# Earlier requests for the first unit's keys and queries, later copies of the first seeds, and a fourth tile for seeds

## The chip, the cores and the metric

The kernel runs on one core of a Trainium2 chip, as one program. The metric is the device time of one execution in microseconds (us). The core has five engines that run side by side: TensorE (PE in the profile; its weight loads are the row PEld), VectorE (DVE), ScalarE (ACT), GpSimd (POOL) and SyncE (SP). In this kernel SP does nothing but ask for DMA transfers, and all of them go through its one queue.

## The reference, cut to what matters

Two independent halves are computed and put side by side. Both have a sequence length of 2048 and a width of 448.

```python
# half A: a state space convolution
P = exp((A * dt)[:, :, None] * pos)           # 448 channels x 256 states x 2048 positions
K = 2 * einsum("dn,dnl->dl", C, P).real       # one filter per channel
y = irfft(rfft(u) * rfft(K))[:2048] + u * D_skip
# half B: attention with 16 heads of 28
q, k, v = split(x @ wqkv)
o = softmax(q @ k.T * 28**-0.5) @ v
out_b = o @ wo
```

## The kernel before, in words

The program has two stages. The first one, the projection stage (the program's loop `for t in range(n_stage)`, line 530), makes two things side by side:

- The products x @ wqkv, in 48 jobs: four chunks of 512 rows, and in each chunk the keys and queries of four groups of four heads and four pieces of v. A job (`qk_proj`, line 448) has 12 matmuls. Its result is split into a high and a low part, tile `hl` (two buffers), by one ACT and one DVE instruction, and stored in HBM (`k<-hl`, `q<-hl` in the profile). The split and the store of a job are written into the program after the matmuls of the job behind it. In the last chunk the keys and queries of group 0 come as jobs 40 and 41, of group 1 as 42 and 43, of group 2 as 44 and 45, of group 3 as 46 and 47.
- The seeds of the filters, from `seeds(o)` for o = 0 to 7 (line 313): few powers of the exponentials, for 7 blocks of 8 channels each. The first half of a set is built in a tile `se`, which is one of three buffers that carry the name `qhat`; POOL clears a part of it with a memset (`places`, line 359) and fills it, and `put_e` stores it (`sd<-qhat`). `put_g` stores the other half (`sd<-sg`).

The loop runs over steps t = 0 to 40. Step t takes the projection jobs that are due (all are done by t = 36), the pieces of the seeds of that step, and the requests in `ahead[t]`. Those requests are for the first attention unit (group 0, first 512 queries): its key differences `kdif` (`load_kd`, 16 transfers of 64 KB), its queries `qhat` (`load_q(0)`, four of 256 KB) and its keys `khat` (`load_k(0, j)`, one head j at a time, four of 256 KB for each). The buffer of the keys of group 0 holds the projection weights until then: the keys of head j lie where the weights of group j were.

After the loop come the maxima of unit 0: for each of 16 pieces of 128 queries, four matmuls (`max_mm`, line 173). The first is reduced by a Relu on ACT (tile `rl`), the second together with that tile by a DVE instruction, the third and fourth by one DVE reduction each. `max_join`, `max_end` and `max_put` write the result into the queries (`qhat<-mh`).

The second stage is the attention loop over 256 steps of 128 keys. In each step four score matmuls (`pss`) go to four exponentials on ACT (`p`) and four product matmuls (`po`). Woven into it are the maxima of the next unit, which run three pieces (LEAD) ahead, and half A: 56 blocks of filters. For a block b the seeds are loaded (`load_sd`, tile `sdb`), copied by ACT into tiles `e` and `g` (`k_seeds`, two calls), multiplied up to all powers by nine POOL instructions for `e` and nine steps on DVE for `g`, and joined by matmuls (`pm<-e,g`). `k_next` asks for the seeds of a later block once the powers of a block are done.

The order of instructions on an engine is set in two ways. In the projection stage and the maxima of unit 0 nothing is pinned (`KEPT["p"]` is empty): the framework's planner orders each engine's instructions by their place in the program and by when it reckons them ready. From line 861 on all five engines keep the order of the program. Tiles of one name share its buffers, and a new tile waits until the last use of the tile before it in that buffer is over.

Of the kernel before, what the change touches and what calls it, by code (L numbers as in the profile page):

```python
# [8 lines left out]
F32 = mybir.dt.float32  # L9
F32R = mybir.dt.float32r  # L10
I32 = mybir.dt.int32
AF = mybir.ActivationFunctionType
# [28 lines left out]
PS = 1  # L41
SGB, XB, XL = 2, 5, 4
K0, KP, KD, UP = 0, 3.5, 4, 3
A0, A1, KW = 26, 34, (33, 35, 36)

N1 = 32
N2 = 64
# [3 lines left out]
NB = D // 8  # L51
# [7 lines left out]
SDF = F_Z + 18 * 16  # L59
# [31 lines left out]
def body(ctx, tc, a, out):  # L91
    nc = Engines(tc)
# [4 lines left out]
    def pool(stack, name, bufs=1, space=None, side=None):  # L97
        kw = {} if space is None else {"space": space}
        if side:
            kw["side"] = side  # L100
        return stack.enter_context(tc.tile_pool(name=name, bufs=bufs, reuse_waits="tile", **kw))
# [31 lines left out]
    k0_p = pool(k0_st, "k0_p", side="right")  # L133
# [11 lines left out]
    def load_k(g, j, p):  # L145
        if j == 0:
            t = k0_t if g == 0 else p.tile([128, HG, L], F32R, name="khat")
            kt_g[g] = [t[:, i] for i in range(HG)]
        for r in range(4):
            nc.sync.dma_start(kt_g[g][j][32 * r:32 * r + 32, :].bitcast(F32), k_d[g][r % 2, 32 * j:32 * j + 32, :])  # L150
# [3 lines left out]
    def load_v(g, c):  # L154
        v_g[g, c] = t = v_p.tile([128, NK // NQ, HG, 32], F32, name="v", bufs=5)
        nc.sync.dma_start(t.rearrange("p t h e -> p t (h e)"), v_d[c][:, g])
# [8 lines left out]
    def load_q(u, rows=range(4)):  # L165
        g, c = divmod(u, NQ)
        if 0 in rows:
            q_u[u] = q_p.tile([128, HG, CQ], F32R, name="qhat", bufs=3)
        t = q_u[u]
        for r in rows:  # L170
            nc.sync.dma_start(t[32 * r:32 * r + 32].bitcast(F32), q_d[g][c][r // 2].rearrange("(j p) q -> p j q", j=HG))

    def max_mm(u, i, kc, ps=w_tile):

        if i == 0 and kc == 0:
            m_u[u] = q_p.tile([128, HG, 4, 3], F32, name="mx", bufs=2)
        j, t = divmod(i, 4)
        pm = ps()
        q, kt = q_u[u][:, j, t * 128:(t + 1) * 128], kt_g[u // NQ][j]
        mx = m_u[u][:, j, t, max(kc - 1, 0):max(kc - 1, 0) + 1]  # L180
        if kc == 0:
            nc.tensor.matmul(pm, q, kd_g[u // NQ, j], start=True, stop=True)
            rl_u[u, i] = kd_p.tile([128, CQ], F32, name="rl", bufs=2)
            nc.scalar.activation(rl_u[u, i], pm, AF.Relu)
        elif kc == 1:
            kb = kt.rearrange("p (c s n) -> p c s n", c=NQ, s=2)[:, :2, 1, :]
            nc.tensor.matmul(pm.rearrange("p (c n) -> p c n", c=2), q, kb, start=True, stop=True)
            rl = rl_u.pop((u, i))
            nc.vector.tensor_tensor_reduce(rl, pm, rl, 1.0, -3.0e38, ALU.add, ALU.max, mx)
        else:  # L190
            nc.tensor.matmul(pm, q, kt[:, kc * CQ:(kc + 1) * CQ], start=True, stop=True)
            nc.vector.tensor_reduce(mx, pm, axis=AX.X, op=ALU.max)

    def max_join(u):
        m_u[u, 1] = q_p.tile([128, HG * 4], F32, name="m1", bufs=2)
        nc.vector.tensor_reduce(m_u[u, 1], m_u[u].rearrange("p a b c -> p (a b) c"), axis=AX.X, op=ALU.max)

    def max_end(u, ps):
        nc.tensor.transpose(ps[:16, :128], m_u[u, 1], ident)
        mh = q_p.tile([16, 2, 128], F32R, name="mh")  # L200
        nc.vector.tensor_scalar(mh[:, 0, :], ps[:16, :128], -1.0, None, op0=ALU.mult)
        nc.vector.scalar_tensor_tensor(mh[:, 1, :], ps[:16, :128], -1.0, mh[:, 0, :].bitcast(F32),
                                       op0=ALU.mult, op1=ALU.subtract)
        mh_u[u] = mh
# [7 lines left out]
    with ExitStack() as st:  # L212
# [47 lines left out]
        t = a["A_log_dt"]  # L260
# [6 lines left out]
        half_pi = s_p.tile([128, 1], F32, name="half_pi")  # L267
# [245 lines left out]
        ahead = collections.defaultdict(list)  # L513
# [2 lines left out]
        for i in range(2):  # L516
            ahead[A1 + i].append(lambda i=i: load_q(0, range(2 * i, 2 * i + 2)))

        for j, t in enumerate(KW):
            ahead[t].append(lambda j=j: load_k(0, j, k0_p))  # L520

        def project():

            e = work.pop(0)() if work else None
            while pend:
                pend.pop(0)()
            if e:
                pend.append(e)

        for t in range(n_stage):  # L530
            while work and n_work - len(work) < n_work * (t + 1) / PW:
                project()
            for f in slots[t] + ahead.get(t, []):
                f()
            if t + 1 == PW:
                project()
                wst.close()
                load_k(0, HG - 1, k0_p)
                load_q(1)
                for c in range(NQ):  # L540
                    load_v(0, c)
        xst.close()
        more = [lambda: ps_t.tile([128, CQ], F32, name="pt")] * 2 + [w_tile] * 3
        for i in range(16):
            for kc in range(4):
                max_mm(0, i, kc, more[(4 * i + kc) % 5])
        max_join(0)
        max_end(0, ps_t.tile([128, CQ], F32, name="pt"))
        max_put(0)
# [6 lines left out]
    g_p = pool(g_st, "g_p")  # L556
# [56 lines left out]
    sds, egs = {}, {}  # L613

    def load_sd(b):
        sds[b] = g_p.tile([128, SDF], F32, name="sdb", bufs=3)
        nc.sync.dma_start(sds[b], sd_d[b // BO][b % BO])

    def k_seeds(b):

        if b not in es:
            es[b] = e = g_p.tile([128, 2, 16, N2], F32, name="e", bufs=2)
            nc.scalar.activation(e[:, :, :, :8], sds[b][:, :F_G].rearrange("p (c h e) -> p c h e", c=2, e=8), AF.Copy)
        else:
            g = g_p.tile([128, 2, 16, N1], F32, name="g", bufs=2)
            nc.scalar.activation(g[:, :, :, :4], sds[b][:, F_G:F_Z].rearrange("p (c h e) -> p c h e", c=2, e=4), AF.Copy)
            egs[b] = es.pop(b), g
# [231 lines left out]
        return spectrum(f, i, p, uh_p, ps, b0) if kind == "s" else finish(f, i, p, ps, b1)  # L859

    nc.kept = KEPT["a"]
    load_sd(0)
    load_sd(1)
    k_seeds(0)
    k_seeds(0)
    for i in range(LEAD):
        for kc in range(4):
            max_mm(1, i, kc)

    urgent, back = collections.deque(), collections.deque()  # L870
    powers = {"g": collections.deque(), "e": collections.deque()}
# [113 lines left out]
    last = [None]  # L985

    def k_next():

        if last[0] is not None and not powers["e"] and not powers["g"]:
            if last[0] + 2 < NB:  # L990
                load_sd(last[0] + 2)
            last[0] = None

    def vec():
# [4 lines left out]
    for s in range(NS):  # L999
# [26 lines left out]
        for op in ORDER:  # L1026
            if op[0] == "s":
                ps.append(s_mm(u, kt, int(op[1])))
            elif op[0] == "f":
                slot(s)  # L1030
            elif op[0] == "v":
                vec()
            elif op == "k":
                k_next()
                k_begin(s)
                k_seed(s)
                for _ in range(3):
                    if powers["e"]:
                        powers["e"].popleft()()
            elif op == "pv":  # L1040
                if prev:
                    pv_step(*prev)
                    if prev[1] == NK - 1:
                        fin(prev[0], s)
            elif sm < NS:
                max_mm(sm // NK, sm % NK, int(op[1]))
        for _ in range(FX if late[0] else 0):
            slot(s)
        if sm < NS and sm % NK == NK - 1:
# [3 lines left out]
            max_join(sm // NK)  # L1053
            soon_slot(UG[0], end)
        k_next()
        prev = (u, kt, ps)
    pv_step(*prev)
# [65 lines left out]
```

## Time and profile before

| | us |
|---|---|
| median of three runs | 1332.18 |
| lowest and highest | 1330.11 and 1336.95 |
| the profiled execution | 1331.76 |
| its span, first to last instruction | 1329.9 |

The span lies 1.9 us below the profiled execution's own time. All instructions are recorded on one line of the code (L75, a helper), so they are told apart by their tiles: `hl<-pm` is what writes tile `hl` from tile `pm`. In the timelines a row has the start and the length in us, the engine, the operation, the tile that is written and those that are read, the shapes and a count; in brackets stands the idle time of that engine before it, and what ended it. SPq is SP asking for a transfer, not the transfer itself.

### The profile page before, as it was taken

The numbers are of one execution on the slowest core, as the hardware profiler recorded it, in microseconds if no ns is written. First come the engines' busy times: TensorE is split into PE (matmuls) and PEld (weight loads), VectorE is DVE, ScalarE is ACT, GpSimd is POOL, SyncE is SP. The second block draws the span as 40 slices with busy tenths as digits, with TensorE's granted clock in tenths as the row PEclk, the third lists the DMA queues.
The fourth block names the chain that finished last, engine by engine and source line by source line (L and its number), as shares of the span: only waits on it lengthen the run. The fifth ranks groups of instructions, "written<-read, shape, count | busy, mean of one in ns | idle before, by whom it ended". The sixth has DMA issues, their size and how long they took to land.

```text
span 1329.9 us, 33195 instructions
## 1 busy us (share of the span) xinstructions
PE 1235.2 (93%) x12625; PEld 705.0 (53%) x12625; DVE 990.1 (74%) x2138; ACT 953.2 (72%) x2067; POOL 838.4 (63%) x704
## 2 busy tenths in 40 slices
PE   6878885699999999999999999999999999898997
PEld 5656763355555555555555555555555545444433
DVE  5897786787777887787788988888886858757311
ACT  4876762388888888888888888888886656555553
POOL 2686681378788788888779999989992202211211
PEclk9989888799999999999999999999999999999999
DMA  6677669725856546468634233732415553825485
GB/s 188 207 272 264 217 211 287 206 57 122 191 134 152 128 129 163 135 165 235 172 95 95 61 72 89 165 78 69 100 50 148 192 157 134 263 102 162 150 217 140
DMA packets 200088, 205.36 MB, mean 154 GB/s; under 512 B 95992, under 2 KB 158520, under 8 KB 197880
## 3 DMA queue, kind: packets, MB, share of 16 engines
q1 hardware_dynamic: 199928, 203.23, 55.1%
q8 instruction: 100, 1.64, 0.5%
q14 instruction: 60, 0.49, 0.1%
HBM read 120.73 MB, written 82.18 MB: 153 GB/s over the span
## 4 chain that ended last, share of the span: by engine, by line
PE 69%; DVE 14%; DMA 5%; ACT 5%; POOL 4%; issue 2%; SPq 1%; ACTq 0%; POOLq 0%; DVEq 0%
PE pm L75 39%; PE pss L75 15%; PE po L75 15%; DVE mx L75 2%; DVE p L75 2%; DVE tri L75 2%; DVE pr L75 1%; POOL qhat L75 1%; ACT p L75 1%; DVE rl L75 1%; DVE sg L75 1%; DVE qhat L75 1%; ACT tri L75 1%; DMA qhat<-q 1%; DVE px L75 1%
## 5 line engine op out<-in xcount | busy, mean ns | idle before, releaser
L75 ACT ACTIVATE p<-pss 128x512 f32<-128x512 f32 x1024 | 561.6, 611 | 118.7 <-PE pss L75 114.3
L75 PE MATMUL pss<-qhat,khat 128*128 128x512 f32 x1024 | 403.3, 400 | 3.8 <-ACT p L75 3.7
L75 DVE TENSOR_REDUCE mx<-pm 128x1 f32<-128x512 f32 x500 | 321.5, 684 | 102.4 <-PE pm L75 100.9
L75 PE MATMUL pm<-khat,qhat 128*128 128x512 f32 x749 | 326.9, 439 | 19.3 <-DVE mx L75 6.7
L75 POOL TENSOR_TENSOR e<-e,sdb 128x256 f32<-128x256 f32 x168 | 201.8, 1201 | 126.7 <-ACT e L75 107.8
L75 PE MATMUL po<-p,v 128*32 128x512 f32 x2048 | 269.9, 596 | 0.0
L75 POOL TENSOR_TENSOR e<-e,eu 128x256 f32<-128x256 f32 x168 | 248.1, 1477 | 13.2
L75 PEld LDWEIGHTS pm<-khat,qhat 128*128 128x128 f32 x749 | 141.5, 189 | 215.1 <-ACT p L75 47.0
L75 DVE CUSTOM_DVE_ANT_0 rl<-pm,rl 128x512 f32<-128x512 f32 x249 | 171.5, 689 | 66.0 <-ACT rl L75 62.2
L75 PEld LDWEIGHTS pss<-qhat,khat 128*128 128x128 f32 x1024 | 190.6, 188 | 50.8 <-ACT p L75 12.4
L75 POOL TENSOR_TENSOR eu<-e,sdb 128x256 f32<-128x256 f32 x168 | 202.0, 1202 | 0.0
L75 POOL TENSOR_TENSOR p<-pr,pr 64x448 f32<-64x448 f32 x32 | 40.9, 1278 | 197.3 <-DVE pr L75 186.3
L75 DVE TENSOR_TENSOR g<-g,zg 128x128 f32<-128x128 f32 x392 | 162.1, 414 | 4.0 <-ACT zg L75 0.6
L75 ACT ACTIVATE rl<-pm 128x512 f32<-128x512 f32 x249 | 151.1, 607 | 16.8 <-PE pm L75 16.8
L75 PE MATMUL pm<-xh,khat 112*128 112x512 f32 x256 | 92.3, 444 | 21.3 <-DVE hl L75 9.8
L75 PE MATMUL pm<-kdif,qhat 128*128 128x512 f32 x249 | 100.9, 405 | 2.3 <-DVE mx L75 1.3
L75 DVE TENSOR_TENSOR zg<-g,zg 128x128 f32<-128x128 f32 x224 | 87.9, 392 | 5.1
L75 PEld LDWEIGHTS pm<-e,g 128*32 128x32 f32 x3584 | 57.6, 110 | 44.0 <-issue 17.8
L75 PE MATMUL pm<-e,g 128*32 128x64 f32 x3584 | 73.7, 222 | 1.9 <-POOL e L75 1.9
L75 ACT ACTIVATE y<-pm 128x448 f32<-128x448 f32 x48 | 26.3, 549 | 65.9 <-issue 32.8
L75 PEld LDWEIGHTS pm<-xh,khat 112*128 112x128 f32 x256 | 53.4, 213 | 36.6 <-DVE hl L75 11.2
L75 PEld LDWEIGHTS po<-p,v 128*32 128x32 f32 x2048 | 55.8, 110 | 22.4 <-issue 17.9
(134 smaller groups left out, 1503.9 us busy)
## 6 DMA issues: line engine op xcount, KB each, us to landing
sdb<-sd SPq DMA_DIRECT2D x56, 336.0 KB
khat<-k SPq DMA_DIRECT2D x64, 256.0 KB
qhat<-q SPq DMA_DIRECT2D x64, 256.0 KB
sd<-sg SPq DMA_DIRECT2D x8, 1456.0 KB
k<-hl SPq DMA_DIRECT2D x16, 512.0 KB
q<-hl SPq DMA_DIRECT2D x16, 512.0 KB
mw<-in_mw SPq DMA_DIRECT2D x16, 512.0 KB
sd<-qhat SPq DMA_DIRECT2D x8, 896.0 KB
```

Of the source, the lines that this page charges most:

```text
L75: i = f(*args, **kw)
```

## The change

There are five edits:

1. The requests for `kdif` move from steps 26 to 33 to steps 16 to 23, those for `qhat` of unit 0 from steps 34 and 35 to steps 24 and 25.
2. The requests for the keys of heads 0, 1 and 2 stay at steps 33, 35 and 36, but stand at the front of their step, ahead of its projection jobs, instead of behind its pieces of seeds.
3. Behind the last maximum of unit 0 stands an additional exponential of one number on ACT (`half_pi`, which nothing reads any more).
4. The two calls `k_seeds(0)`, which copy the first seeds on ACT, move behind the twelve `max_mm(1, ...)` that come ahead of the loop.
5. `sdb` has four buffers instead of three; three blocks are loaded ahead of the loop instead of two, and `k_next` asks for block b + 3 instead of b + 2.

```diff
-A0, A1, KW = 26, 34, (33, 35, 36)
+A0, A1, KW = 16, 24, (33, 35, 36)
...
-        for j, t in enumerate(KW):
-            ahead[t].append(lambda j=j: load_k(0, j, k0_p))
+        firsts = {t: lambda j=j: load_k(0, j, k0_p) for j, t in enumerate(KW)}
...
         for t in range(n_stage):
+            if t in firsts:
+                firsts[t]()
             while work and n_work - len(work) < n_work * (t + 1) / PW:
                 project()
...
                 max_mm(0, i, kc, more[(4 * i + kc) % 5])
+        nc.scalar.activation(half_pi[:1], half_pi[:1], AF.Exp)
         max_join(0)
...
-        sds[b] = g_p.tile([128, SDF], F32, name="sdb", bufs=3)
+        sds[b] = g_p.tile([128, SDF], F32, name="sdb", bufs=4)
...
-    load_sd(0)
-    load_sd(1)
-    k_seeds(0)
-    k_seeds(0)
+    for b in range(3):
+        load_sd(b)
     for i in range(LEAD):
         for kc in range(4):
             max_mm(1, i, kc)
+    k_seeds(0)
+    k_seeds(0)
...
-            if last[0] + 2 < NB:
-                load_sd(last[0] + 2)
+            if last[0] + 3 < NB:
+                load_sd(last[0] + 3)
```

## The prediction

> **What bounds the kernel now.** I read the stretches of the span first, to see where an engine is not full. (Columns: the stretch; busy us and count of PE, PEld, DVE, ACT, POOL; granted clock, DMA share, GB/s.)
>
> ```profile
> span 1329.9 us, 33195 instructions
> PE 1235.2 (93%) x12625; PEld 705.0 (53%) x12625; DVE 990.1 (74%) x2138; ACT 953.2 (72%) x2067; POOL 838.4 (63%) x704
> ...
> 210.00:240.00 30.00, 21.17 (x52) 10.59 (x53) 22.56 (x49) 9.09 (x17) 0.00 (x0) 0.84 1.05 272
> 240.00:270.00 30.00, 21.39 (x68) 10.12 (x67) 21.78 (x51) 12.81 (x26) 12.55 (x11) 0.79 0.59 170
> ...
> 300.00:340.00 40.00, 39.76 (x509) 22.14 (x511) 31.14 (x75) 33.42 (x76) 34.30 (x28) 1.00 0.61 138
> ```
>
> From 300 on PE is full (39.76 of 40 us): the attention loop goes at PE's pace, so it ends as much sooner as it starts sooner. Between 210 and 270, where the projections give way to the loop, no engine is full, and from 210 to 240 the DMA engines are (1.05). All but one of the edits act there or feed it. So the question is when the maxima of unit 0 start, and when the loop does.
>
> Second, the chain of work that ended last, for the transfers on it before the loop:
>
> ```profile
> 119.78 6.49 DMA k<-hl
> ...
> 194.90 2.87 DMA q<-hl
> ...
> 203.16 11.80 DMA qhat<-q
> ...
> 249.75 3.07 DMA sdb<-sd
> ```
>
> Two hold a whole engine back: the 11.80 us for the first queries, ahead of the maxima, and the seeds, ahead of the loop. The timelines show what stands around the first (SPq: requests):
>
> ```profile
> 184.39 1.24 SPq L75 DMA_DIRECT2D sd<-qhat  x1
> ...
> 196.75 1.75 SPq L75 DMA_DIRECT2D khat<-k  x4
> 198.96 0.39 SPq L75 DMA_DIRECT2D k<-hl  x1
> ...
> 201.19 0.42 SPq L75 DMA_DIRECT2D q<-hl  x1
> ...
> 203.21 0.40 PE L75 MATMUL pm<-xl,khat 112*128 112x512 f32 x1
> 215.10 0.77 PE L75 MATMUL pt<-kdif,qhat 128*128 128x512 f32 x1 [11.49 <-DMA qhat<-q]
> ...
> 205.16 0.69 ACT L75 ACTIVATE hl<-pm,kones 128x512 fp32r<-128x512 f32 x1 [6.68 <-DMA k<-hl]
> ...
> 210.28 0.63 ACT L75 ACTIVATE hl<-pm 128x512 fp32r<-128x512 f32 x1
> ...
> 210.94 0.69 DVE L75 TENSOR_TENSOR hl<-pm,hl 128x512 fp32r<-128x512 f32 x1 [1.05 <-ACT hl L75]
> 216.53 0.69 DVE L75 CUSTOM_DVE_ANT_0 rl<-pt,rl 128x512 f32<-128x512 f32 x1 [4.90 <-ACT rl L75]
> ```
>
> The last projection matmul ends at 203.61. PE then waits 11.49 us for queries. But the queries are not all: ACT stands 6.68 us before the split of the keys of group 3 (205.16), because the store of group 2's keys (198.96) has yet to free one of the two `hl` buffers, and it lies behind the 1 MB of head 0's keys asked for at 196.75. The last split ends on DVE at 211.63, the first DVE work of the maxima starts at 216.53.
>
> **Term 1, the start of the maxima (edits 1 and 2).** With `kdif` gone, SP comes to head 0's keys right behind the `sd<-qhat` of 184.39, at 185.63, which is 11 us sooner. The store of 198.96 then has no megabyte ahead of it; I give it the 2.87 us of the `q<-hl` at 194.90. It lands at 201.8, and the split of 205.16 moves up by 3.3. From there to the end of the last split was 211.63 - 205.16 = 6.5 us. That split needs the buffer of the store of 201.19, which now has head 1's megabyte ahead; 198.96 to 205.16, 6.2 us, is what a store took behind a megabyte, so this split starts at 207.4 instead of 207.0 (210.28 less 3.3), and ends on DVE at 208.7. Queries and head 0's keys have long landed, and PE and the Relu of the first piece run while the last split does. So the maxima's first DVE work is at 208.7: **7.8 us gained**. Bounds: if the last split stays where it is, 216.53 - 211.63 = 4.9; if the planner puts the first pieces straight behind the last projection matmul, 203.61 plus the 1.43 us from PE's 215.10 to 216.53 gives 205.0, a gain of 11.5. The maxima themselves keep their pace, three DVE instructions for each piece.
>
> **Terms 2 and 3, from the maxima to the loop (edits 3 and 4).**
>
> ```profile
> 252.98 0.42 ACT L75 ACTIVATE e<-sdb 128x256 f32<-128x256 f32 x1 [8.57 <-DMA sdb<-sd]
> 253.30 0.29 ACT L75 ACTIVATE g<-sdb 128x128 f32<-128x128 f32 x1
> 253.50 0.58 ACT L75 ACTIVATE rl<-pm 128x512 f32<-128x512 f32 x1
> ...
> 258.00 0.60 ACT L75 ACTIVATE rl<-pm 128x512 f32<-128x512 f32 x1 [1.71 <-PE pm L75]
> 260.00 0.60 ACT L75 ACTIVATE rl<-pm 128x512 f32<-128x512 f32 x1 [1.40 <-PE pm L75]
> 260.62 1.28 ACT L75 ACT_TABLE_LOAD   x1
> 261.91 0.60 ACT L75 ACTIVATE p<-pss 128x512 f32<-128x512 f32 x1
> ...
> 248.06 0.47 PE L75 MATMUL pm<-kdif,qhat 128*128 128x512 f32 x1
> ```
>
> The first piece of unit 1 is out of PE at 248.53, but its Relu starts at 253.50, since ACT stands in order behind the copy `e`, which waits for seeds (8.57 us). With the copies behind the three pieces the Relu starts at 248.6: **4.9 us**. What is then late? The three Relus end at 258.60 - 4.9 = 253.7; the seeds land at 249.75 + 3.07 = 252.8 on the same scale, since their request stays behind `max_put`; so the copies (0.71 us) find them there, and fit into the 1.40 us that ACT waited ahead of the Relu of 260.00. Should the seeds land later than 253.7, the rest of that wait comes back. Bounds 3.0 (they land 2 us later) to 4.9.
>
> The table load of 260.62 is the exponentials' table and stands on the path, with PE's score matmuls done ahead of it. The added exponential takes it to where ACT is idle, behind the last Relu of unit 0: **1.3 us**, bounds 0 (the planner moves it and it is paid elsewhere) to 1.3. The Trainium skill ("ScalarE: Activation LUTs", What ACT_TABLE_LOAD costs) puts a drain of 1.38 us beside each load; by it this term would be 2.7. The trace disagrees: the Relu ends at 260.60 and the exponential starts at 261.91, so the row's 1.28 is all there is.
>
> POOL's cover: the powers of block 0 start with the copy `e`, so they start 0.8 us later on the clock of the maxima, 0.8 + 6.2 = 7.0 later against the loop.
>
> ```profile
> 262.93 2.39 POOL L75 TENSOR_TENSOR e<-e,eu 128x1024 f32<-128x1024 f32 x1
> ...
> 274.50 0.65 PE L75 MATMUL pm<-e,g 128*32 128x64 f32 x32
> ```
>
> They ended at 265.32 and were wanted at 274.50: 9.2 us of cover, 2.2 left. If it were gone, PE would wait in step 4 for the difference.
>
> **Term 4, seeds three blocks ahead (edit 5).** In the loop, the list of waits has
>
> ```profile
> ACT e L75 <- DMA sdb<-sd: 2.9, 5, 1.1
> ```
>
> 2.9 us in five waits. A request one block sooner ends them; as PE is full there, I take **1.0**, bounds 0 to 2.9.
>
> **What is paid: earlier transfers (edit 1).** The requests `sd<-qhat` of sets 1, 2 and 3 stand in steps 16, 20 and 24.
>
> ```profile
> 87.62 1.07 SPq L75 DMA_DIRECT2D sd<-qhat  x1
> ...
> 117.58 0.86 SPq L75 DMA_DIRECT2D sd<-qhat  x1
> ...
> 132.12 0.45 SPq L75 DMA_DIRECT2D sd<-qhat  x1
> ...
> 110.00:115.00 5.00, 2.24 (x15) 1.56 (x14) 4.53 (x11) 3.38 (x10) 4.16 (x5) 1.00 1.02 336
> ...
> 130.00:135.00 5.00, 5.00 (x23) 4.04 (x22) 3.74 (x7) 4.97 (x10) 4.28 (x8) 1.00 1.03 368
> 135.00:140.00 5.00, 3.52 (x25) 2.63 (x24) 4.93 (x15) 3.72 (x12) 4.05 (x4) 1.00 0.47 158
> ```
>
> So steps 16 to 25 are about 88 to 137 us. The DMA engines are full from 110 to 135, at 336 to 368 GB/s. Six `kdif` transfers (0.39 MB) go ahead of the store of 119.78, whose 6.49 us are on the chain: 0.39 MB at 336 GB/s is **1.2 us lost**. The queries (1 MB) come at 132 to 137, where the share falls to 0.47, and are hidden. Bounds 0 and 6.2 (all of the 2.1 MB). A rule of the Trainium skill speaks against this edit: on each DMA engine descriptors are consumed in ring order ("DMA: Bandwidth & Descriptors", Queues, rings and completion order). By it alone everything behind pays all 2.1 MB, 6.2 us, and the sum below would lose 5 more. That the queue runs empty after 135 is why I don't take it.
>
> **What is paid: a buffer (edit 1).** The queries take one of the three `qhat` buffers ten steps sooner, so the seeds' `se` tiles have two.
>
> ```profile
> 125.08 0.56 POOL L75 MEMSET qhat<- 128x112 f32 x2 [0.91 <-DMA sd<-qhat]
> ...
> 145.74 0.50 POOL L75 MEMSET qhat<- 128x112 f32 x2
> 152.26 0.98 POOL L75 TENSOR_TENSOR gz<-tri 128x224 f32<-128x224 f32 x1 [6.01 <-ACT tri L75]
> ...
> 163.42 0.57 SPq L75 DMA_DIRECT2D sd<-qhat  x1
> ```
>
> The memsets of sets 5 and 6 (125.08, 145.74) then wait for the stores of sets 3 and 4, asked for at 132.12 and 163.42, instead of those of 2 and 3. What was seen of such a wait is 0.91 us; I take **1.0 lost** for two of them, bounds 0 and what the second rival gives.
>
> **The sum.** 7.8 + 4.9 + 1.3 + 1.0 - 1.2 - 1.0 = 12.8. From the profiled execution's 1331.76 (span 1329.9 and 1.9 around it; 0.4 below the median) that gives **1319.0 us**.
>
> **The rivals.**
>
> *The gain at the maxima is eaten (1325.6).* Head 0's megabyte now goes ahead of the stores of group 1, and the requests of heads 1 and 2 go ahead of those of groups 2 and 3. If each store lands later by what a megabyte costs, the last split stays near 211.6, the first term falls to its 4.9, and with the full 6.2 us for the moved transfers it is gone. Terms 2 and 3 alone give 1331.76 - 6.2. For it: the DMA share is 1.05. Against: the megabyte of the queries has left this stretch.
>
> *Slower: POOL stands at a memset (1338 to 1343).* If the planner leaves the memset of set 6 where it stands now, ahead of POOL's work of 152.26, POOL waits there for the store of 163.42. The store of 117.58 was waited for until 125.08, 7.5 us, so that is 170.9, 19.1 us after 152.26, and set 5, behind it, holds up the ACT and DVE instructions that the projections share. 1319.0 + 19.1 = 1338.1; with the full queue price, 1343. It decides the sign from a wait of 13 us on. Against it: the planner moves a memset behind the freeing of its buffer, as it did at 125.08, and misses by 1 us.
>
> *More (1311).* The planner starts the maxima between the last projections (11.5 for 7.8), nothing is paid, and term 4 is 2.9: 7.8 more, 1311.2.
>
> *The edit does nothing* is possible for the table load alone: -1.3.
>
> **How the numbers follow.** My sum 0.53, gain eaten 0.20, more 0.13, slower 0.14. The range goes from 1311, the end of the better case, to 1336, past the eaten case with its lost terms and short of most of the memset's. A measurement of this kernel tells 0.5% (6.7 us, thus 1325.5) from no change. Faster: 0.52 of the first, 0.13, and nearly half of the second (which lies at the bound): 0.73. Slower: the upper part of the second rival, above 1338.8, 0.10. The rest, 0.17, is the same.
>
> **What would show it.** Right: `kdif` and the first `qhat` requests before 140; PE's pause ahead of the first `pt<-kdif,qhat` down from 11.49 to under 5 us, and that matmul before 209; no table load between the last Relu and the first `p`; `e<-sdb` behind three Relus with next to no wait; first `p` about 13 us sooner than 261.91. Wrong: a POOL memset with a wait of over 5 us; a `k<-hl` or `q<-hl` that ACT waits for longer than 7 us; DMA waits within the maxima of unit 0; PE waiting for `e` in the loop's first steps.

## The result and the profile after

The changed kernel is a little slower: 1336.38 us (median of 16 runs, 1333.86 to 1342.14) against 1332.18 us before (16 runs beside them), a ratio of 1.0032 with a 95% interval of 1.0018 to 1.0045. The forecast of 1319.0 us is wrong, in size and in sign. The profiled execution has a span of 1332.4 us against 1329.9; as a whole it took 1334.17 us, 2.2 below the median.

First the stretches (columns as in the prediction), one row of before that was not shown yet and then those of after:

```profile
150.00:180.00 30.00, 27.52 (x125) 23.15 (x124) 22.35 (x39) 22.63 (x44) 21.08 (x23) 0.90 0.59 183
```

```profile
span 1332.4 us, 33199 instructions
...
110.00:150.00 40.00, 33.60 (x146) 27.13 (x147) 31.33 (x51) 26.43 (x45) 22.42 (x23) 0.87 0.64 210
150.00:180.00 30.00, 16.22 (x72) 12.94 (x71) 17.19 (x30) 19.11 (x35) 17.11 (x19) 0.72 0.62 181
180.00:210.00 30.00, 23.73 (x107) 18.78 (x107) 18.17 (x34) 19.39 (x40) 18.50 (x22) 1.00 0.94 291
210.00:240.00 30.00, 23.48 (x57) 13.56 (x55) 22.84 (x49) 8.06 (x18) 7.75 (x10) 0.77 0.76 232
240.00:270.00 30.00, 25.42 (x69) 12.72 (x69) 26.36 (x61) 11.62 (x23) 5.91 (x7) 0.83 0.97 270
```

From 150 to 180 all engines do less at once: PE 16.22 us instead of 27.52, DVE 17.19 instead of 22.35. That is the projection stage, ahead of the rows around 200 us on which term 1 rested. And POOL still works after 210 (7.75 us), where it had been done before: the seeds are late.

The end of the path does what was forecast. ACT's timeline of after, from the maxima to the loop:

```profile
209.12 1.28 ACT L75 ACT_TABLE_LOAD   x1
210.41 0.20 ACT L75 ACTIVATE half_pi<-half_pi 1x1 f32<-1x1 f32 x1
...
262.79 0.60 ACT L75 ACTIVATE rl<-pm 128x512 f32<-128x512 f32 x1 [1.70 <-PE pm L75]
263.29 0.41 ACT L75 ACTIVATE e<-sdb 128x256 f32<-128x256 f32 x1
...
265.09 0.60 ACT L75 ACTIVATE rl<-pm 128x512 f32<-128x512 f32 x1 [1.20 <-PE pm L75]
265.59 1.08 ACT L75 ACTIVATE p<-pss 128x512 f32<-128x512 f32 x2
```

The copy `e` finds its seeds there and waits for nothing, no table load stands ahead of the first `p`, and the one that used to is paid at 209.12, where ACT is idle next (4.15 us). But the first `p` starts at 265.59 instead of 261.91. The start of the loop was lost ahead of all this. Three timelines of the projection stage of after show where:

```profile
159.22 2.73 POOL L75 TENSOR_TENSOR tri<-tr,pw 128x1232 f32<-128x1232 f32 x1 [1.28 <-ACT tr L75]
161.89 0.50 POOL L75 MEMSET qhat<- 128x112 f32 x2
...
190.25 2.59 POOL L75 TENSOR_TENSOR tri<-tr,pw 128x1232 f32<-128x1232 f32 x1 [13.31 <-ACT tr L75]
160.84 0.47 PE L75 MATMUL pm<-vh,xl 112*128 112x448 f32 x1
175.04 0.74 PE L75 MATMUL pm<-vh,xh 112*128 112x448 f32 x1 [13.73 <-ACT vst L75]
...
179.69 0.42 PE L75 MATMUL pt<-kdif,qhat 128*128 128x512 f32 x1
189.80 0.93 DVE L75 TENSOR_TENSOR sg<-tri 128x336 f32<-128x336 f32 x2 [15.78 <-DMA sd<-sg]
...
228.87 0.68 DVE L75 TENSOR_TENSOR hl<-pm,hl 128x512 fp32r<-128x512 f32 x1
```

PE stands 13.73 us for a copy of v on ACT (`vst`), DVE 15.78 us for a store of seeds, POOL 13.31 us for ACT. In before, from 150 to 215, only PE's 11.49 us for the queries is longer than the 6.68 us shown for `k<-hl`. The last split of a projection starts on DVE at 228.87 (before: 210.94). That the queries are there early shows in 179.69: the planner even puts the first maxima between the projections. That helps in part: the projections end 17.9 us later, but the maxima, which need the last of them, only 9.7 us later (257.19 instead of 247.47).

Why are they late? SP's timeline, before and after. `nat` are the inputs of a set of seeds (four requests, the first of each shown):

```profile
97.17 0.83 SPq L75 DMA_DIRECT2D nat<-in_A_log_A_real  x1
...
122.75 0.87 SPq L75 DMA_DIRECT2D nat<-in_A_log_A_real  x1
...
140.37 0.83 SPq L75 DMA_DIRECT2D nat<-in_A_log_A_real  x1
```

```profile
110.31 0.87 SPq L75 DMA_DIRECT2D nat<-in_A_log_A_real  x1
...
142.35 0.84 SPq L75 DMA_DIRECT2D nat<-in_A_log_A_real  x1
...
153.71 0.84 SPq L75 DMA_DIRECT2D sd<-qhat  x1
...
160.43 15.11 SPq L75 DMA_DIRECT2D v<-vst  x2
175.63 0.87 SPq L75 DMA_DIRECT2D nat<-in_A_log_A_real  x1
```

The last three sets get their inputs 13, 20 and 35 us later, and the store of set 3 is asked for at 153.71 instead of 132.12. The moved requests stand ahead of them, and so do stores of projections, each of which SP waits for in its order: the pair `v<-vst` holds SP for 15.11 us, because the copy `vst` is in turn late on ACT (it starts at 174.41, and the second request of the pair at 175.02). The transfers' bytes are not it: from 110 to 150 the DMA share is 0.64, against 0.80 before.

### The profile page after: what moved, and what is told of

It is laid out like the page before. It is cut to its first block, busy times and chain, and to the rows that moved or that the text cites. A ratio compares the mean times of both kernels' runs of the same rounds, so it can differ in the third digit from the quotient of the medians.

```text
span 1332.4 us, 33199 instructions
## 1 busy us (share of the span) xinstructions
PE 1237.2 (93%) x12625; PEld 706.5 (53%) x12625; DVE 986.0 (74%) x2138; ACT 956.2 (72%) x2070; POOL 839.3 (63%) x704
## 4 chain that ended last, share of the span: by engine, by line
PE 70%; DVE 13%; POOL 6%; issue 3%; ACT 3%; DMA 3%; SPq 0%; ACTq 0%; POOLq 0%; DVEq 0%
PE pm L75 40%; PE pss L75 15%; PE po L75 15%; DVE mx L75 2%; POOL qhat L75 2%; DVE p L75 2%; POOL e L75 2%; DVE pr L75 1%; DVE tri L75 1%; DMA sd<-qhat 1%; DVE px L75 1%; DVE rl L75 1%; ACT p L75 1%; DVE sg L75 1%; DVE qhat L75 1%
## 5 line engine op out<-in xcount | busy, mean ns | idle before, releaser
L75 PEld LDWEIGHTS pm<-xh,khat 112*128 112x128 f32 x256 | 53.7, 216 | 37.8 <-DVE hl L75 14.4
```

Source lines behind the costliest of these rows:

```text
L75: i = f(*args, **kw)
```

## The experiments

Each kernel was run in five rounds beside the kernel before (e5 in three). Ratios are to that, with their 95% interval.

**The loop edits alone.** e1 has edits 3, 4 and 5, e6 edit 5 alone; the requests stay as before.

> Edits 3, 4 and 5 alone (added exponential, first seeds' copies behind the maxima, seeds three blocks ahead); all requests of the projection stage as before. All theories: the projection stage keeps its times (last reduction of the maxima of unit 0 at about 247), the first exponential of the loop comes 6 us sooner than 261.9, and the time falls by 6 to 8 us, to about 1325. If the gain were an effect of the later start alone (DMA queue empty by then), the seeds would land late here too and the gain would be under 3 us.

> Edit 5 alone (seeds three blocks ahead in four tiles). My sum gave it 1.0 us. The prediction's term: 0 to 3 us faster. Rival (the loop's waits for seeds differ from run to run, 2.9 us in the profile of before, 6 to 7.5 in those with other requests, and PE loses what ACT loses): 3 to 5 us faster, and the loop from its first exponential to its end about 1067 us in every profile.

e1: 1323.48 us, 0.9924 (0.9907 to 0.9941). e6: 1330.59 us, 0.9988 (0.9974 to 1.0003). So edits 3 and 4 are worth what was forecast or more (7.1 us by the difference of the two, as no run has them alone), edit 5 alone is not told from nothing, and the requests turn a gain of 9.4 us into a loss of 4.

**Each moved request alone**, on the kernel before:

```diff
e2  -A0, A1, KW = 26, 34, (33, 35, 36)
    +A0, A1, KW = 16, 34, (33, 35, 36)
e3  +A0, A1, KW = 26, 24, (33, 35, 36)
e4  edit 2 alone: the keys at the front of their steps
e5  the first of the four query requests at step 24, the others at 34 and 35
```

> The kernel before with only the key differences asked for at steps 16 to 23. Theory A (the loss comes from the buffer that the early queries take from the seeds): no change beyond 2 us. Theory B (the loss comes from requests and bytes that go ahead of the stores in SP's queue): 6 to 12 us slower. Theory C (any change of the requests makes the planner order ACT, DVE and POOL anew, and the loss is what that order does on the chip): a change of some us in either direction, with another order of instructions on ACT around 150 to 190.

> The kernel before with only the queries of unit 0 asked for at steps 24 and 25. Theory A: 8 to 14 us slower, POOL's memsets of sets 5 and 6 late (about 160 and 190 instead of 125 and 146), last split of the projections after 220. Theory B: 2 to 5 us slower at most (1 MB moved to a stretch with room). Theory C: some us in either direction.

> The kernel before with only the keys of heads 0 to 2 asked for at the front of their steps. Theories A and B: 0 to 4 us faster or no change (keys earlier, queries still late, so the wait of 11.5 us ahead of the maxima stays up to 9). Theory C: some us in either direction.

> The kernel before, but the first of the four query transfers (256 KB) is asked for at step 24, which takes the buffer ten steps sooner; the other three stay at steps 34 and 35. Buffer theory: as with all four early, POOL's memsets of sets 5, 6 and 7 come at about 147, 185 and 203 and the last split of the projections ends after 216; the maxima still wait for the late queries, so the maxima end at 250 or later, 2 to 6 us slower. Theory of bytes: memsets and splits stay within 2 us of the kernel before, no change.

e2 1336.98 us (1.0024, 1.0008 to 1.0040), e3 1337.53 (1.0032, 1.0020 to 1.0044), e4 1338.49 (1.0035, 1.0018 to 1.0051), e5 1334.58 (1.0021, 1.0003 to 1.0039). No one of the three is the culprit; each loses. The keys in front lose at the queries (SP and PE of e4):

```profile
205.64 2.30 SPq L75 DMA_DIRECT2D qhat<-q  x2
218.96 0.76 PE L75 MATMUL pt<-kdif,qhat 128*128 128x512 f32 x1 [12.80 <-issue]
```

The last queries are asked for 3.4 us later than before (202.28 there), since heads 0 and 1 are asked for ahead of them, and the maxima start 3.9 us later. e5 takes the buffer ten steps sooner and moves few bytes. The memsets of sets 5 and 6 move from 125.08 and 145.74 to 146.72 and 176.45, but the last split stays (it starts at 211.27). The lost buffer by itself delays the seeds, not the projections.

**Adding them up.** With the loop edits kept: e12 puts the keys in front, e11 the queries early too, e8 keys and `kdif`. e9 has the requests without the loop edits; e10 is a control, `kdif` one step later in the kernel before.

```diff
e12 A0, A1 = 26, 34   edits 2 to 5 kept
e11 A0, A1 = 26, 24   edits 2 to 5 kept
e8  A0, A1 = 16, 34   edits 2 to 5 kept
e9  A0, A1 = 16, 24   edits 1 and 2 only
e10 A0, A1 = 27, 34   nothing else
```

> The changed kernel with the queries back at steps 34 and 35: key differences early, keys at the front of their steps, edits 3, 4 and 5. Buffer theory: most of the loss in the projections goes, 1322 to 1327. Theory C: it stays about 1332 or more, since the other two requests cost 4 us each by themselves.

> The kernel before with edits 1 and 2 alone (all the requests of the first unit moved; the loop edits left out). Theory additive (what the requests cost in the projection stage is independent of what the loop edits gain behind it): the loop edits alone brought 9.4 us (1332.9 to 1323.5), so this kernel is 9.4 us above the changed one: about 1345.8, ratio to before 1.010. Rival (the changed kernel's loss comes out of both together, and the requests cost about what the dearest of them costs alone): about 1338, ratio 1.004.

> A control: the kernel before with the sixteen kdif requests one step later (27 to 34), nothing else. By transfers and buffers nothing of weight changes: within 1 us of before, the last split at about 211 us, ratio 1.000. If the planner's order alone makes such shifts (any moved request sorts the projection stage anew), the last split moves by 2 us or more, either way, and the time by as much.

> The changed kernel with kdif back at steps 26 to 33; queries early, keys in front, loop edits kept. By the ends of the maxima of the kernels with one edit, added up (queries +2.2, keys in front +3.1) on the 1323.5 of the loop edits: 1328.8, ratio 0.997. If the queries' buffer, which the seeds lose, is what delays the last projections, kdif matters little: 1335 to 1337, ratio 1.003, with the memset of set 6 behind 184 us and the last split behind 218 us.

> The changed kernel with kdif and queries back at their old steps: only the keys in front and the loop edits are left. By the end of the maxima of the kernel with the keys in front alone (+3.1): 1326.6, ratio 0.995, first queries' wait ahead of the maxima 12 to 13 us. If the keys in front hurt only because they meet something that the loop edits take away: 1323.5, ratio 0.992.

e8 1330.45 us (0.9991, 0.9978 to 1.0004), e9 1346.56 (1.0109, 1.0084 to 1.0135), e10 1331.88 (0.9996, 0.9978 to 1.0013), e11 1329.23 (0.9970, 0.9955 to 0.9986), e12 1326.88 (0.9957, 0.9940 to 0.9974). e9, e11 and e12 came out within 1 us of the sum: what the requests cost and what the loop edits gain add up. For e11 that is partly luck: the queries' 2.2 us were to come from a later end of the maxima, but in its profile they end where those of e12 do (251.32 and 251.47), and the two intervals overlap. e8 fits neither of its theories. The exception to the adding up is `kdif` together with the queries: on the keys in front, `kdif` costs 3.6 us and the queries 2.3, both 9.5.

Late requests alone don't make that loss. In e2 `kdif` is early on SP and the queries stay where they were (SP and DVE):

```profile
142.35 0.84 SPq L75 DMA_DIRECT2D nat<-in_A_log_A_real  x1
...
153.69 0.89 SPq L75 DMA_DIRECT2D sd<-qhat  x1
...
157.66 1.39 SPq L75 DMA_DIRECT2D nat<-in_A_log_A_real  x1
212.00 0.69 DVE L75 TENSOR_TENSOR hl<-pm,hl 128x512 fp32r<-128x512 f32 x1 [1.05 <-ACT hl L75]
```

The inputs of set 6 and the store of set 3 are asked for as late as in the changed kernel, yet the last split starts only 1.1 us later than before. The queries hold no buffer here, and the memset of set 5 stands at 138.50. With the queries early as well it is at 161.89 (changed kernel) and 162.75 (e9).

In e10 the last split moves by 3.4 us (214.30) and the time stays, because PE waits until 215.94 for the queries anyway: shifts of that size are hidden in the kernel before.

**Off SP's queue.** The same requests at the same steps, asked for by another engine:

```diff
e13 -nc.sync.dma_start(...)          # load_kd of group 0 and load_q of unit 0
    +nc.gpsimd.dma_start(...)
e14 +nc.scalar.dma_start(...)
e18 +nc.gpsimd.dma_start(...)        # load_kd only; the queries stay on SP
e17 as e13, without edit 2 (the keys where they were before)
```

> The changed kernel with the early requests (kdif and the queries of unit 0) asked for by GpSimd instead of SP, at the same steps. If SP's one queue is what holds the store of set 3: it is asked for near 132 again instead of 153.7, the memset of set 5 stands near 145 instead of 161.9, PE's wait of 13.7 us for the copy of v is gone, and the time is that of the kernel with kdif late, about 1329 (less what GpSimd pays for 20 requests, so up to 1332). If the lost buffer or the transfers' bytes do it: the memset stays near 160 and the time near 1336.

> The same with ScalarE asking for them. If SP's queue: about 1329 to 1332, the store of set 3 near 132; ScalarE pays for 20 requests, the dearest way. If buffer or bytes: about 1336 or more.

> The changed kernel with kdif alone asked for by GpSimd; the queries stay on SP at steps 24 and 25. If kdif's sixteen requests on SP are what put the store of set 3 to 154: it is near 133, the memset of set 5 near 146, and the time is that of the kernel with kdif late, about 1329. If the queries' requests on SP hold the rest up as well: the memset of set 5 lies behind 155 and the time is about 1333 to 1336.

> The changed kernel with the early requests asked for by GpSimd, and without edit 2 (keys behind the pieces of seeds of their steps, as before). If the keys in front cost here what they cost alone and on top of the loop edits (3.1 to 3.4 us): 1319.5, ratio 0.990. If they cost nothing where the queries have landed long before: 1322.7, ratio 0.993.

e13: 1322.72 us (0.9934, 0.9919 to 0.9949), 13.7 us below the changed kernel, with the same transfers into the same buffers. (GpSimd comes to the `kdif` requests at 76 to 96 and to the queries at 127 to 137; SP did at 96 to 151 and 154 to 160.) e18: 1329.13 (0.9985, 0.9972 to 0.9997). e17: 1319.06 (0.9906, 0.9891 to 0.9922), the fastest of all. SP, POOL and DVE of e13:

```profile
98.81 0.83 SPq L75 DMA_DIRECT2D nat<-in_A_log_A_real  x1
...
124.42 0.87 SPq L75 DMA_DIRECT2D nat<-in_A_log_A_real  x1
...
133.50 1.14 SPq L75 DMA_DIRECT2D sd<-qhat  x1
...
141.54 0.83 SPq L75 DMA_DIRECT2D nat<-in_A_log_A_real  x1
146.78 0.55 POOL L75 MEMSET qhat<- 128x112 f32 x2
215.59 0.69 DVE L75 TENSOR_TENSOR hl<-pm,hl 128x512 fp32r<-128x512 f32 x1 [0.50 <-ACT hl L75]
...
244.30 0.20 DVE L75 TENSOR_REDUCE m<-mx 128x16 f32<-128x48 f32 x1
```

The inputs of the seeds and the store of set 3 are asked for when they were before, within 1.7 us; PE's wait of 13.73 us for `vst` is gone, and the maxima end at 244.30 instead of 257.19. The memset of set 5 stands at 146.78, so the buffer is lost here too, without harm. The bytes do none either: the DMA share from 110 to 150 is 0.95. In e18 only the queries are left on SP:

```profile
154.00 7.16 SPq L75 DMA_DIRECT2D v<-vst  x2
161.25 0.87 SPq L75 DMA_DIRECT2D nat<-in_A_log_A_real  x1
```

They put back only the last of the inputs (140.37 before), and as in the changed kernel a pair `v<-vst` stands ahead of it, for 7.16 us. The kernels with the loop edits in one table (requests and first `p` from their profiles):

| | last two `nat` requests | first `p` | median |
|---|---|---|---|
| e1, requests as before | 123.08, 140.90 | 256.51 | 1323.48 |
| e12, keys in front | 123.14, 140.96 | 259.87 | 1326.88 |
| e11, and queries early | 122.60, 161.22 | 259.72 | 1329.23 |
| e8, keys in front and `kdif` early | 143.37, 159.00 | 262.65 | 1330.45 |
| changed kernel, all three | 142.35, 175.63 | 265.59 | 1336.38 |
| e18, `kdif` by GpSimd | 123.65, 161.25 | 259.17 | 1329.13 |
| e13, `kdif` and queries by GpSimd | 124.42, 141.54 | 253.00 | 1322.72 |
| e17, the same, keys as before | 123.52, 140.63 | 249.71 | 1319.06 |

e14 is the miss: 1335.21 us (1.0028, 1.0013 to 1.0043), although the store of set 3 is at 129.18 and the last inputs at 139.53. Its waits from 80 to 215:

```profile
POOL tri L75 <- ACT tri L75: 20.9, 4, 15.2
DVE xl L75 <- ACT xh L75: 16.1, 3, 14.8
```

Others now wait for ACT, and the last split starts at 230.41. What makes ACT late there (20 requests in its order, or the order that the planner then gave all engines) was not separated. The requests are over at 145.94, and where one stands alone it mostly takes 0.31 us, so they were not the dearest way that I had expected; ACT's own longest wait from 80 to 215, 7.41 us until 157.88, is for a store of v (`v<-vst`). So neither the bytes nor the lost buffer by itself makes the 13.7 us, since both stay in e13; the loss goes together with the delays in SP's order. But e13 also asks sooner, through a queue of its own, and with another order by the planner on all engines, and e14 has SP's requests back in time and loses all the same. That SP's order alone makes the 13.7 us is therefore not shown.

**Keys and queries in the loop.** The loop edits with other steps for the late requests:

```diff
e7  A1 = 32, KW = (33, 35, 36)
e15 A1 = 32, KW = (35, 36, 37)
e16 A1 = 32, KW = (36, 37, 38)
```

> Edits 3, 4 and 5 with the queries asked for at steps 32 and 33 instead of 34 and 35, behind set 6 of the seeds, so that the seeds keep the buffers that they had. Buffer theory: projections as in the kernel before, the queries land ahead of head 0's keys and the maxima start 2 to 5 us sooner than 217: 1319 to 1321. Theory C (any moved request costs through the planner's new order): 1326 or more.

> The loop edits, queries at steps 32 and 33, and the keys of heads 0 to 2 at steps 35, 36, 37 instead of 33, 35, 36. If a megabyte of keys ahead of a store in the one queue costs what the keys in front showed (about 3 us at the maxima's end), the last split comes 2 to 3 us sooner and the time is about 1320. If the wait for the keys themselves takes its place: 1322.4 or more, with PE waiting for khat before or within the maxima of unit 0.

> As the one before, with the keys at steps 36, 37, 38. If the queue: 1318 to 1320, last split near 209. If the keys are then late: PE waits for khat, by up to the 11 us that a megabyte of queries took behind the others, and the time is 1325 to 1330.

e7 1322.43 us (0.9937, 0.9916 to 0.9958), between its two theories and not to be told from e1. e15 1340.70 (1.0070, 1.0056 to 1.0084) and e16 1341.90 (1.0073, 1.0056 to 1.0090): keys one to three steps later than in e7 lose 18 and 19 us, more than either expectation had. PE of e15, within the maxima of unit 0:

```profile
248.74 1.19 PE L75 MATMUL pm<-khat,qhat 128*128 128x512 f32 x2 [13.52 <-DMA khat<-k]
```

One of the theories had a gain here, and the last split does come sooner in e15 (212.77 instead of 214.27 in e7). But the keys of the first head are asked for at 207.27 instead of 196.98, those of the last at 235.60 instead of 219.75, behind the next unit's queries and v. In front the keys hold up the queries and the stores, behind they are waited for.

## Why the prediction was wrong

**The step that failed is term 1, with the two prices that went with it** (7.8 - 1.2 - 1.0 = 5.6 us to be gained). Measured, edits 1 and 2 cost 13.8 us without the loop edits (e9, 1346.56 against 1332.77) and 12.9 with them (1336.38 against 1323.48); of the 12.9, the keys in front (edit 2) make 3.4 (e12) and the early requests (edit 1) 9.5. I moved the rows around 200 us by hand and left all that lies ahead of them in its place. The last split was to end at 208.7 instead of 211.63; it ends at 229.55. Of the requests, `kdif` came at 96 to 151 and the queries at 154 to 160, not before 140, and head 0's keys at 198.94 instead of the 185.63 of the forecast.

**The price of the earlier transfers was worked out for the wrong resource.** 1.2 us was six transfers' bytes, 6.2 the bound with all of them. What the requests took, by the traces, was their place in SP's order, ahead of the seeds' inputs and stores. The trace of before had the rows for it: `nat` at 97.17, 122.75 and 140.37, in and right behind the 88 to 137 us that I gave the steps to which the requests were moved. The first of them even stands on the chain that ended last (`97.17 1.24 DMA nat<-in_A_log_A_real`), ahead of the rows of it that I showed. I named the queue's stores `k<-hl` and never asked whose requests the moved ones pass. By the Trainium skill ("DMA: Bandwidth & Descriptors", Queues, rings and completion order) I had put the loss from ring order at 5 more; the 20 us by which the inputs of 122.75 come later arise before their request, so the order in which requested transfers are served is not what makes them late. The Trainium skill also says ("DMA: Bandwidth & Descriptors", Issuing engines are not separate DMA queues) that issuing from several engines saves only the issue time, usually small beside the transfer. Here issuing from GpSimd saved 13.7 us, while the 16 `kdif` requests took it 8.7 us (550 ns each): by the request times, the saving was in what stands behind a request, not in the request.

**The buffer** was priced at 1.0 us. The shift of the memsets came (from 125.08 to 146.72 in e5, 146.78 in e13), not as waits, since the planner moved them. It costs the projections nothing alone. With `kdif` on SP as well, the store that frees the buffer is late too, and the memset is at 161.89; that fits the extra 3.6 us of the two together, and PE's wait for `vst`, which e9 has too and e8 and e11 have not at that length. The store's delay is shown. That the buffer carries it on to PE was not tested by itself; e2, with the late store and the buffer free, speaks for it.

**The rivals.** The slower case (1338 to 1343, from a wait of POOL at the memset of set 6) came nearest in sign and size: set 5 did hold up the instructions that the projections share. But its mechanism, an unmoved memset, was not it, and it came near by luck. (Its 170.9 lies 18.7 us behind 152.26, not 19.1.) The case of eaten gains, which by its own terms comes to 1326.9 and not 1325.6 (4.9 - 6.2 is a loss of 1.3, not nothing), is visible as well: ACT waits 5.04 us for `k<-hl` at 223.39, against none ahead of the last split of e17, where the keys are not in front. That the planner would start maxima between the projections, my better case, did happen (179.69), and in e13 and e17, where nothing holds the projections, it brought a gain, if less than the 7.8 of the sum or the 11.5 of that case: the maxima end 3.8 and 6.8 us sooner than in e1 (248.11).

**The signs.** None of the signs of being wrong marks the loss: no memset on POOL waits longer than 1.34 us, ACT's longest wait for `k<-hl` is 5.04 us, no instruction of the maxima waits for a transfer, and up to 300 PE waits for `e` only 0.2 us. Three of the signs of being right are there: no pause ahead of the first `pt<-kdif,qhat`, at 179.69, no table load ahead of the first `p`, and no wait of `e<-sdb`. The signs came from the same rows as term 1 and could not show what failed ahead of them.

**Terms 2 and 3 were right.** From the end of the maxima to the first `p` it took 261.91 - 247.47 = 14.4 us before and 265.59 - 257.19 = 8.4 after: 6.0 gained of the 6.2 forecast; 8.4 in e1 and in e17 too. The load had no drain beside it (0.01 us to the next instruction). The moved load adds none (15 in before and in e1); early requests on SP do, by the planner's new order: 17 in the changed kernel, e2 and e11.

**Term 4 was too small, or before's profile too kind.** In the loop ACT waits for seeds, list of waits of e2 (no edit 5):

```profile
ACT e L75 <- DMA sdb<-sd: 7.5, 6, 2.8
```

The profiles of the other kernels without edit 5 (e3 to e5, e9, e10) have 5.5 to 7.3 us, before's 2.9 is the lowest; none with it shows such a wait. From the first `p` to the end of the span it is 1068.0 us in before, 1069.1 to 1073.8 in those without edit 5, and 1066.3 to 1068.7 in those with it. That may be what makes e1's 9.4 us more than the 7.2 forecast (terms 2 to 4); its own profile doesn't show it, with the first `p` 5.4 us sooner and a span 6.4 shorter, and e6, edit 5 alone, doesn't show it with certainty. It also means that in the profiles the costs of e2 to e4 lie only in part ahead of the loop (first `p` 1.1, 2.5 and 3.4 us later than before).

**The number 1319.0 itself** was reached by e17 (1319.06), with the loop edits' 9.4 us and the requests of edit 1 on another queue. Its interval overlaps that of e1, so what the early requests add there, 4 us by the medians, is likely and not certain. That it meets the forecast is luck in part: the forecast had 7.2 us from the loop edits and 5.6 from the requests. A gain of the forecast's size was to be had, not by the edit as it was written.

## What to carry to other kernels

Before a request is moved up, list every request that it passes on its issuing engine, and for each what hangs on it: loads of another stream and stores that free a buffer count, and so does what that engine will then wait for in its order. A delay that hardly moves the rows behind it by itself, as that of the inputs in e2 (last split 1.1 us later), may cost much when a second change comes on top. The bytes were the smaller part here; where early requests are wanted, a second queue on an engine that has room keeps them out of the way, and a run has to tell which engine that is. Where a planner orders the instructions, a hand-moved row holds only as long as nothing ahead of it is touched.

## What was not expected of the hardware

- The same 20 requests cost 13.7 us more on SP than on GpSimd (1336.38 against 1322.72), while ScalarE was no better than SP (1335.21).
- A single pair of requests held SP for 15.11 us, because the data to be stored weren't ready; what stood behind it was asked for that much later.
- Keys asked for 5 to 16 us later (e15 against e7) cost 18 us: within the maxima, PE waited 13.52 us at once.
